# First chunk of a relu² attention and hard-swish MLP kernel: z and v are fetched ahead of the stores, ScalarE rounds v, and GpSimd's queue fetches the weights

## The chip, the cores and the metric

The kernel runs on one core of one Trainium2 chip. The metric is the device time of an execution in microseconds (us), and lower is better. Three runs of the kernel before took 1998.2, 1998.15 and 1996.16 us, a median of 1998.15 us. One more execution was profiled.

The engines go by the names of the profile. PE is TensorE (PEld its weight loads), DVE is VectorE, ACT is ScalarE, POOL is GpSimd, and SP is SyncE, which here only issues DMAs. Each engine, and each queue that issues DMAs, works through its own list of instructions in order.

## The reference

The computation has two stages, and the output of the first is the input of the second:

```python
B, S, D, DQK, DFF = 4, 3008, 256, 64, 2048
scores = (1.0 / S) * np.matmul(z, z.transpose(0, 2, 1))
attn = np.maximum(scores, 0.0) ** 2
x = (u * np.matmul(attn, v)).reshape(B * S, D)
h = x @ w_in
g = h * np.clip(h + 3.0, 0.0, 6.0) / 6.0
out = g @ w_out
```

u, v and z are float32. The two weight matrices arrive as float64 and are read as pairs of 32-bit words.

## The kernel before

**Precision.** Every operand of a matmul is kept as two float32r parts, a rounded high part (names that end in h) and the rest (l), and every product is taken as three matmuls: l by h, h by l, h by h. `split` makes the parts: ACT rounds the high part with a copy, and DVE subtracts it from the raw value. For z the parts lie in one tile each: `zx` and `zy` hold the high part in one half of the partitions and the rest in the other.

**Chunks and pairs.** For each of the four batches the 3008 columns of the scores are cut into six chunks `c` of 512 columns (the last has 448), so there are 24 chunks, and the 3008 rows into twelve pairs `p` of 2 x 128 rows. `scores(b, c, p)` makes one pair: four matmuls `s<-...` into one of two PSUM buffers, Relu on ACT (`rt`, L320), its square rounded on ACT (`ah`, L329), in the first chunk its unrounded square also on ACT (`r`, L330), and the rest on DVE (`al`, L340). `attend` (function `av`) then multiplies with v: twelve matmuls `o<-...`. The scores are symmetric: what is needed again in a later chunk is stored to DRAM by `keep` (`d<-r`, L257, two DMAs of a pair), and for the later chunk it comes back by four loads (`l<-d`, L240) and a transpose on DVE (`rm`, L271) in place of matmuls.

**The MLP** is cut into units, `up(q)` (twelve matmuls `h<-...`) and `down(q)` (twelve matmuls `y<-...`) for q = 0 to 7 of each chunk. They begin at pair 28 of all, counted from 0 (`FIRST = 28`, in the third chunk), and follow the attention of the pairs in a fixed proportion of about 1.4 units to a pair. The units of the first chunk come in the order up 0, up 1, down 0, up 2, down 1, ... up 7, down 6, down 7.

**The weights** come in sixteen pieces (w_in 0 to 7 and w_out 0 to 7, in the order in which the units of the first chunk use them). A piece is fetched by one 512 KB DMA (`wraw`, L152), and eight DVE instructions and one ACT copy turn it into its two parts: L101, L106, L110, L114, L119 and L123, and then, after the same six of the next piece, L131 and L133. This work is a generator, and the main loop takes some steps of it at a time:

```python
def weight_work(n):
    for _ in range(n):
        next(w_ops, None)

def weight_needed(w):
    while w not in ready:
        next(w_ops)
```

`weight_work` stands ahead of `attend` in every pair: 2 steps in the first chunk, 4 in the next, 5 from pair 28 of all on. `weight_needed` stands ahead of each unit of the first chunk and takes whatever steps are missing until the unit's piece is done.

**What sets the order.** The program order is written out by hand (`tc.manual_schedule()`), and each engine gets its instructions in that order. Tiles wait for the last users of their buffer: the pool `rpool` (tag `r`) has five buffers for `rt`, `r`, `rm`, `y` and the two `wraw` in flight. A DMA on SP's queue is issued once the eighth DMA before it on that queue has landed.

**The first chunk** (L561 to L608) has loads that later chunks do not have: z and v of batch 0. `fetch_z(0, k)` loads a raw z chunk through SP; for k > 1 two more loads through POOL's queue bring the high parts, which a DMA from float32 to float32r rounds. `fetch_v(0, p)` loads raw v through SP and a second, rounded copy `vh` through POOL's queue. The fetches run up to four pairs ahead of their use and stand between the stores of `keep`. Before the loop the first two weight pieces are fetched (`weight_work(1)`).

Of the kernel before, what the change touches and what calls it, by code (L numbers as in the profile page):

```python
# [15 lines left out]
P = 128  # L16
CH = 512
NCH = 6
# [12 lines left out]
def relu2_attention_then_hswish_mlp(  # L31
# [43 lines left out]
    def split(hi, lo, raw, rounded=False):  # L75
        if not rounded:
            nc.scalar.copy(out=hi, in_=raw)  # L77
        nc.vector.tensor_tensor(out=lo, in0=raw, in1=f(hi), op=ALU.subtract)  # L78
# [69 lines left out]
    def fetch_w(kind, q):  # L148
        _, _, src, cols = w_piece(kind, q)
        if wide:  # L150
            raw = rpool.tile([P, 2, D, 2], U32, tag="r", name="wraw")
            nc.sync.dma_start(  # L152
                out=raw.rearrange("p k n w -> p k (n w)"),
                in_=src[:, :, 2 * cols.start:2 * cols.stop],
            )
        else:
            raw = rpool.tile([P, 2, D], F32, tag="r", name="wraw")
            nc.sync.dma_start(out=raw, in_=src[:, :, cols])
        raws["w", kind, q] = raw

    raws = {}
# [3 lines left out]
    def fetch_v(b, p):  # L165

        if b == 0 and p < NPAIR - 1:
            raw = vpool.tile([P, 2, D], F32, tag="vl", name="vraw")
        else:
            raw = stg.tile([P, 2, D], F32, tag="stg", name="vraw")  # L170
        vh = vpool.tile([P, 2, D], F32R, tag="vh", name="vh")
        vt[b, p] = vh
        raws["v", p] = raw
        j0 = p * 2 * P
        for dst, queue in ((raw, nc.sync), (vh, nc.gpsimd))[:1 if b else 2]:
            if p < NPAIR - 1:
                queue.dma_start(
                    out=dst, in_=v[b, j0:j0 + 2 * P, :].rearrange("(r q) d -> q r d", q=P)
                )
            else:  # L180
                queue.dma_start(out=dst[:, 0, :], in_=v[b, j0:j0 + P, :])
                for h in range(2):
                    queue.dma_start(out=dst[64 * h:64 * h + 64, 1, :], in_=v[b, j0 + P:S, :])

    def split_v(b, p):
        vh, raw = vt[b, p], raws.pop(("v", p))
        vl = vpool.tile([P, 2, D], F32R, tag="vl", name="vl")
        split(vh, vl, raw, rounded=b == 0)
        vt[b, p] = (vh, vl)

    def fetch_z(b, k):
# [327 lines left out]
# [3 lines that stand above are left out]
# [39 lines left out]
    with tc.manual_schedule():  # L561
# [3 lines left out]
        split_z(0, 0)  # L565
        fetch_z(0, 1)
        fetch_v(0, 1)
        weight_work(1)
        split_v(0, 0)
        split_z(0, 1)  # L570
        scores(0, 0, 0)
        fetch_z(0, 2)
        fetch_v(0, 2)
        scores(0, 0, 1)
        fetch_v(0, 3)
        g_done = 2
        to_fetch += [(b, c, p) for b, c, p in pairs if p // 2 < c]
        g_turned = [2]
        for i, (b, c) in enumerate(chunks):
            ahead = b + 1 if c == NCH - 1 and b + 1 < B else None  # L580
            for p in range(NPAIR):
                g = i * NPAIR + p
                lead = 2 if g < FIRST else 1
                if i == 0:
                    if p + 1 < NPAIR:
                        split_v(0, p + 1)
                    if p % 2 == 0 and p // 2 + 2 < NCH:
                        split_z(0, p // 2 + 2)
# [4 lines left out]
                    fetch_mirrored()  # L593
                if p < NPAIR - 1:
                    turn_next()
                if i == 0:
                    if p + 4 < NPAIR:
                        fetch_v(0, p + 4)
                    if p % 2 == 0 and p // 2 + 3 < NCH:
                        fetch_z(0, p // 2 + 3)  # L600
                    if p == 6:
                        load_u(*chunks[0])
                        load_u(*chunks[1])
                maybe_split()
                if g >= FIRST:
                    weight_work(5)
                elif p < NPAIR - 2:
                    weight_work(4 if i else 2)  # L608
                if ahead and p < NPAIR - 1:
                    if p:  # L610
# [61 lines left out]
```

## Time and profile before

| | |
|---|---|
| Median of three runs | 1998.15 us |
| The profiled execution | 1999.87 us, of which 1998.1 us lie between its first and last instruction (the span) |
| PE busy in the span | 1960.8 us, 98% |
| DVE, ACT, POOL busy | 1280.7, 987.3 and 14.2 us |
| Mean granted clock of PE | 0.992 of full speed |
| Data moved by DMA | 178.14 MB |

The profile counts PE as busy while a matmul is in flight, and the matmuls overlap, so the count of matmuls in a stretch (the x behind the busy time) says more than the busy time. At full clock one matmul with 512 columns follows another after 0.227 us (twelve in 2.72 us), so 50 us have room for 220. The granted clock has two levels, 2.4 GHz (1.00) and 1.2 GHz (0.50); a stretch with both shows a value between. In the timeline a row gives the start, the duration, the engine, the line, the tiles, and in brackets how long the engine was idle ahead of it and who ended that. Rows of SPq are DMA issues on SP's queue.

### The profile page before, as it was taken

The numbers are of one execution on the slowest core, as the hardware profiler recorded it, in microseconds if no ns is written. First come the engines' busy times: TensorE is split into PE (matmuls) and PEld (weight loads), VectorE is DVE, ScalarE is ACT, GpSimd is POOL, SyncE is SP. The second block draws the span as 40 slices with busy tenths as digits, with TensorE's granted clock in tenths as the row PEclk, the third lists the DMA queues.
The fourth block names the chain that finished last, engine by engine and source line by source line (L and its number), as shares of the span: only waits on it lengthen the run. The fifth ranks groups of instructions, "written<-read, shape, count | busy, mean of one in ns | idle before, by whom it ended". The sixth has DMA issues, their size and how long they took to land.

```text
span 1998.1 us, 22059 instructions
## 1 busy us (share of the span) xinstructions
PE 1960.8 (98%) x8688; PEld 1637.4 (82%) x8688; DVE 1280.7 (64%) x1277; ACT 987.3 (49%) x1057; POOL 14.2 (1%) x26
## 2 busy tenths in 40 slices
PE   7899999999999999999999999999999999999999
PEld 5677788788888888888888888888888888888888
DVE  6798766676556566577565565657756565665654
ACT  6665444465444444456454454444555544444444
POOL 2000000000000000000000000000000000000000
PEclk8899999999999999999999999999999999999999
DMA  9754232424323233253332232324342223332300
GB/s 260 201 159 110 64 82 71 113 74 116 82 64 81 72 74 93 51 127 91 95 82 82 62 90 56 98 65 106 93 116 61 83 61 92 74 82 60 94 10 20
DMA packets 403271, 178.14 MB, mean 89 GB/s; under 512 B 250080, under 2 KB 385248, under 8 KB 403168
## 3 DMA queue, kind: packets, MB, share of 16 engines
q1 hardware_dynamic: 399232, 172.55, 34.3%
q0 software_dynamic: 3936, 4.20, 1.0%
q8 instruction: 68, 1.11, 0.2%
q14 instruction: 35, 0.29, 0.1%
HBM read 104.07 MB, written 72.61 MB: 88 GB/s over the span
## 4 chain that ended last, share of the span: by engine, by line
PE 89%; DVE 4%; DMA 3%; ACT 2%; issue 1%; SPq 1%; DVEq 0%; ACTq 0%
PE o L73 34%; PE h L73 24%; PE y L73 24%; PE s L73 7%; DMA zraw<-in_zz_dram 1%; DVE rm L271 1%; DMA vraw<-in_v_dram 1%; DVE al L287 1%; DVE rt L421 1%; ACT rt L420 0%; SPq L240 0%; ACT gh L77 0%; ACT rt L320 0%; DVE gl L78 0%; DMA d<-r 0%
## 5 line engine op out<-in xcount | busy, mean ns | idle before, releaser
L421 DVE SCALAR_TENSOR_TENSOR rt<-rt,h 128x1024 f32<-128x1024 f32 (+1 forms) x192 | 229.9, 1197 | 419.9 <-ACT rt L420 419.6
L420 ACT ACTIVATE rt<-h,three 128x1024 f32<-128x1024 f32 (+1 forms) x192 | 210.9, 1099 | 548.4 <-PE h L73 545.6
L73 PE MATMUL o<-ah,vl 128*128 128x512 f32 (+1 forms) x1152 | 448.5, 389 | 9.7 <-DVE vl L78 3.7
L73 PE MATMUL o<-ah,vh 128*128 128x512 f32 (+1 forms) x1152 | 447.6, 389 | 0.0
L73 PE MATMUL o<-al,vh 128*128 128x512 f32 (+1 forms) x1104 | 430.3, 390 | 7.8 <-DVE al L287 6.4
L73 PE MATMUL y<-gh,w_out_l 128*128 128x512 f32 (+1 forms) x768 | 296.2, 386 | 1.8 <-DVE w_out_l L133 1.7
L73 PE MATMUL y<-gl,w_out_h 128*128 128x512 f32 (+1 forms) x768 | 296.3, 386 | 1.0 <-DVE gl L78 1.0
L73 PE MATMUL h<-xh,w_in_l 128*128 128x512 f32 (+1 forms) x768 | 295.9, 385 | 0.0
L73 PE MATMUL y<-gh,w_out_h 128*128 128x512 f32 (+1 forms) x768 | 295.9, 385 | 0.0
L73 PE MATMUL h<-xl,w_in_h 128*128 128x512 f32 (+1 forms) x768 | 295.8, 385 | 0.0
L73 PE MATMUL h<-xh,w_in_h 128*128 128x512 f32 (+1 forms) x768 | 295.8, 385 | 0.0
L78 DVE TENSOR_TENSOR gl<-rt,gh 128x1024 fp32r<-128x1024 f32 (+1 forms) x192 | 230.6, 1201 | 80.5 <-ACT gh L77 77.9
L73 PEld LDWEIGHTS o<-ah,vl 128*128 128x128 f32 x1152 | 218.4, 190 | 57.6 <-ACT ah L285 5.8
L77 ACT CAST gh<-rt 128x1024 fp32r<-128x1024 f32 (+1 forms) x192 | 197.2, 1027 | 123.5 <-DVE rt L421 123.3
L73 PEld LDWEIGHTS o<-ah,vh 128*128 128x128 f32 x1152 | 218.6, 190 | 40.9
L73 PEld LDWEIGHTS o<-al,vh 128*128 128x128 f32 x1104 | 209.2, 190 | 51.5 <-DVE al L287 9.8
L320 ACT ACTIVATE rt<-s 128x1024 f32<-128x1024 f32 x168 | 171.2, 1019 | 131.9 <-PE s L73 126.9
L332 DVE TENSOR_TENSOR r<-rt 128x1024 f32<-128x1024 f32 (+1 forms) x140 | 169.9, 1214 | 95.8 <-ACT rt L320 95.8
L340 DVE TENSOR_TENSOR al<-r,ah 128x1024 fp32r<-128x1024 f32 x140 | 170.9, 1221 | 22.2 <-ACT r L330 8.7
L73 PEld LDWEIGHTS y<-gh,w_out_l 128*128 128x128 f32 x768 | 144.2, 188 | 29.9 <-DVE w_out_l L133 1.3
L73 PEld LDWEIGHTS y<-gl,w_out_h 128*128 128x128 f32 x768 | 144.2, 188 | 28.6 <-DVE gl L78 2.0
L287 DVE TENSOR_TENSOR al<-rm,ah 128x1024 fp32r<-128x1024 f32 (+1 forms) x120 | 141.1, 1176 | 40.0 <-ACT ah L285 39.9
(51 smaller groups left out, 1808.7 us busy)
## 6 DMA issues: line engine op xcount, KB each, us to landing
d<-r SPq DMA_DIRECT2D x220, 256.0 KB, 2.9
l<-d SPq DMA_DIRECT2D x320, 128.0 KB, 3.2
l<-d SPq DMA_DIRECT2D x160, 112.0 KB, 2.8
vraw<-in_v_dram SPq DMA_DIRECT2D x44, 256.0 KB, 3.4
u<-in_ut_dram SPq DMA_DIRECT2D x20, 512.0 KB, 4.3
out_dram<-y SPq DMA_DIRECT2D x40, 256.0 KB, 3.2
zraw<-in_zz_dram SPq DMA_DIRECT2D x24, 256.0 KB, 3.7
wraw<-in_w_in_dram SPq DMA_DIRECT2D x8, 512.0 KB, 4.5
```

Source lines behind the costliest of these rows:

```text
L73: nc.tensor.matmul(out, lhsT=lhsT, rhs=rhs, start=start, stop=stop)
L77: nc.scalar.copy(out=hi, in_=raw)
L78: nc.vector.tensor_tensor(out=lo, in0=raw, in1=f(hi), op=ALU.subtract)
L271: nc.vector.transpose(out=rn.rearrange("p r (k e) -> p r k e", e=32), in_=t[:, :n // 32].rearrange("p k (r e) -> p r k e", r=2),)
L287: nc.vector.tensor_tensor(out=al[:, :, :n], in0=rn, in1=f(ah[:, :, :n]), op=ALU.subtract)
L320: nc.scalar.activation(out=rn, in_=s[:, :, :n], func=AF.Relu, scale=1.0 / S)
L332: nc.vector.tensor_tensor(out=r2_of, in0=r_of, in1=r_of, op=ALU.mult)
L340: nc.vector.tensor_tensor(out=l_of, in0=r2_of, in1=h_of, op=ALU.subtract)
L420: nc.scalar.activation(out=rn, in_=h, func=AF.Relu, bias=three)
L421: nc.vector.scalar_tensor_tensor(out=rn, in0=rn, scalar=6.0, in1=h, op0=ALU.min, op1=ALU.mult)
```

## The change

It has four parts. (1) In the first chunk `fetch_v` no longer loads the rounded copy `vh` through POOL's queue; `split_v` lets ACT round it, as in the later batches. (2) z 2 and 3 and v 2 and 3 are fetched ahead of the first scores, z 4 and 5 at the start of pairs 0 and 1, and v 4 and later at the start of the pair, all ahead of that pair's stores. (3) The sixteen weight loads go through POOL's queue. (4) `weight_work(1)` before the loop is gone, and pair 0 of the first three chunks takes no step of the weights' work (`0 < p`). Loads of u move from pair 6 to pair 7.

```diff
@@ fetch_w
-            nc.sync.dma_start(
+            nc.gpsimd.dma_start(
                 out=raw.rearrange("p k n w -> p k (n w)"),
                 in_=src[:, :, 2 * cols.start:2 * cols.stop],
             )
...
@@ fetch_v
-        for dst, queue in ((raw, nc.sync), (vh, nc.gpsimd))[:1 if b else 2]:
-            if p < NPAIR - 1:
-                queue.dma_start(
-                    out=dst, in_=v[b, j0:j0 + 2 * P, :].rearrange("(r q) d -> q r d", q=P)
-                )
...
+        if p < NPAIR - 1:
+            nc.sync.dma_start(
+                out=raw, in_=v[b, j0:j0 + 2 * P, :].rearrange("(r q) d -> q r d", q=P)
+            )
...
@@ split_v
-        split(vh, vl, raw, rounded=b == 0)
+        split(vh, vl, raw)
@@ main
         fetch_v(0, 1)
-        weight_work(1)
+        fetch_z(0, 2)
+        fetch_z(0, 3)
+        fetch_v(0, 2)
+        fetch_v(0, 3)
         split_v(0, 0)
         split_z(0, 1)
         scores(0, 0, 0)
-        fetch_z(0, 2)
-        fetch_v(0, 2)
         scores(0, 0, 1)
-        fetch_v(0, 3)
...
                 if i == 0:
+                    if p + 4 < NPAIR:
+                        fetch_v(0, p + 4)
+                    if p < 2:
+                        fetch_z(0, p + 4)
...
-                if i == 0:
-                    if p + 4 < NPAIR:
-                        fetch_v(0, p + 4)
-                    if p % 2 == 0 and p // 2 + 3 < NCH:
-                        fetch_z(0, p // 2 + 3)
-                    if p == 6:
-                        load_u(*chunks[0])
-                        load_u(*chunks[1])
+                if i == 0 and p == 7:
+                    load_u(*chunks[0])
+                    load_u(*chunks[1])
                 maybe_split()
                 if g >= FIRST:
                     weight_work(5)
-                elif p < NPAIR - 2:
+                elif 0 < p < NPAIR - 2:
                     weight_work(4 if i else 2)
```

PE's instructions stand in the same order as before. The change moves instructions on DVE, ACT, SP and POOL; the three places that the prediction speaks of follow.

On ACT, in the middle of the first chunk, the list before goes as follows (rt, ah and r are one pair's scores, w_in_h is a weight piece):

```order
L320 ACTIVATE rt<-s 128x1024
L329 ACTIVATE ah<-rt 128x1024
L330 ACTIVATE r_263<-rt 128x8x4x32
L117 CAST w_in_h<-t_198 128x2x256
L320 ACTIVATE rt<-s 128x1024
L329 ACTIVATE ah<-rt 128x1024
L330 ACTIVATE r_306<-rt 128x8x4x32
```

The same stretch of ACT's list now (the line numbers behind the change are one lower):

```order
L77 CAST vh<-vraw 128x512
L319 ACTIVATE rt<-s 128x1024
L328 ACTIVATE ah<-rt 128x1024
L329 ACTIVATE r_309<-rt 128x8x4x32
L77 CAST vh<-vraw 128x512
L319 ACTIVATE rt<-s 128x1024
L328 ACTIVATE ah<-rt 128x1024
L329 ACTIVATE r_346<-rt 128x8x4x32
```

One rounding of v has come in for every pair.

On DVE, early in the fourth chunk's attention, where the first chunk's last MLP units run, the list before goes as follows (rt and gl belong to the unit up 7, the steps of the weights' work finish the piece w_out 6; the piece w_in 7 was finished in the stretch ahead of this one):

```order
L271 STREAM_TRANSPOSE rm<-l 128x1024
L114 SCALAR_TENSOR_TENSOR t_1590<-wraw,t_1590 128x512
L119 TENSOR_SCALAR wraw<-t_1590 128x512
L123 SCALAR_TENSOR_TENSOR w_out_l<-wraw 128x512
L131 TENSOR_TENSOR t_1490<-t_1490,w_out_h 128x512
L133 TENSOR_TENSOR w_out_l<-t_1490,w_out_l 128x512
L421 SCALAR_TENSOR_TENSOR rt<-rt,h 128x1024
```

The same place of DVE's list now:

```order
L270 STREAM_TRANSPOSE rm<-l 128x1024
L101 TENSOR_SCALAR t_1623<-wraw 128x512
L106 SCALAR_TENSOR_TENSOR t_1623<-wraw,t_1623 128x512
L110 TENSOR_SCALAR wraw<-wraw 128x512
L114 SCALAR_TENSOR_TENSOR t_1623<-wraw,t_1623 128x512
L119 TENSOR_SCALAR wraw<-t_1623 128x512
L123 SCALAR_TENSOR_TENSOR w_out_l<-wraw 128x512
L131 TENSOR_TENSOR t_1504<-t_1504,w_in_h 128x512
L133 TENSOR_TENSOR w_in_l<-t_1504,w_in_l 128x2x256
L101 TENSOR_SCALAR t_1657<-wraw 128x512
L420 SCALAR_TENSOR_TENSOR rt<-rt,h 128x1024
```

Nine steps stand where five stood: `weight_work` takes five, and `weight_needed`, called for the unit up 7, four more, and among them are now those that finish w_in 7.

One pair later on DVE, ahead of the unit down 6, the list before (xl are the parts of the next chunk's x, the two steps finish w_out 7):

```order
L271 STREAM_TRANSPOSE rm<-l 128x1024
L78 TENSOR_TENSOR xl_1701<-u,xh_1700 128x512
L78 TENSOR_TENSOR xl_1705<-u,xh_1704 128x512
L131 TENSOR_TENSOR t_1590<-t_1590,w_out_h 128x512
L133 TENSOR_TENSOR w_out_l<-t_1590,w_out_l 128x512
L287 TENSOR_TENSOR al<-rm,ah 128x1024
```

The same place now:

```order
L270 STREAM_TRANSPOSE rm<-l 128x1024
L78 TENSOR_TENSOR xl_1691<-u,xh_1690 128x512
L78 TENSOR_TENSOR xl_1695<-u,xh_1694 128x512
L106 SCALAR_TENSOR_TENSOR t_1657<-wraw,t_1657 128x512
L110 TENSOR_SCALAR wraw<-wraw 128x512
L114 SCALAR_TENSOR_TENSOR t_1657<-wraw,t_1657 128x512
L119 TENSOR_SCALAR wraw<-t_1657 128x512
L123 SCALAR_TENSOR_TENSOR w_out_l<-wraw 128x512
L131 TENSOR_TENSOR t_1623<-t_1623,w_out_h 128x512
L133 TENSOR_TENSOR w_out_l<-t_1623,w_out_l 128x512
L131 TENSOR_TENSOR t_1657<-t_1657,w_out_h 128x512
L286 TENSOR_TENSOR al<-rm,ah 128x1024
```

Eight steps stand where two stood, and the seventh of them finishes w_out 6.

## Rows read from the trace of the kernel before

**Rows 1.** The view of stretches over the whole span: the stretch, PE's busy time (instructions), the same of PEld, DVE, ACT and POOL, then PE's granted clock, the DMA share and GB/s.

```profile
0.00:50.00 50.00, 37.77 (x133) 29.18 (x134) 29.99 (x41) 31.60 (x34) 14.21 (x26) 0.86 1.13 260
50.00:100.00 50.00, 42.70 (x165) 33.74 (x164) 38.04 (x53) 31.53 (x34) 0.00 (x0) 0.86 0.70 201
...
200.00:300.00 100.00, 96.94 (x423) 78.57 (x422) 67.16 (x66) 45.34 (x47) 0.00 (x0) 1.00 0.32 73
```

**Rows 2.** The timeline of PE in the first chunk, the matmuls ahead of which PE stood idle longest.

```profile
32.01 0.47 PE L73 MATMUL s<-zy,zx 128*128 128x512 f32 x1 [2.28 <-issue]
34.98 0.77 PE L73 MATMUL o<-ah,vl 128*128 128x512 f32 x1 [1.49 <-DVE vl L78]
...
54.89 0.77 PE L73 MATMUL s<-zy,zx 128*128 128x512 f32 x1 [3.90 <-issue]
...
72.16 0.47 PE L73 MATMUL o<-ah,vl 128*128 128x512 f32 x1 [2.21 <-DVE vl L78]
```

**Rows 3.** The timeline of DVE, the two splits of z that waited longest.

```profile
30.50 0.68 DVE L78 TENSOR_TENSOR zy<-zraw,zx 64x512 fp32r<-64x512 f32 x1 [4.74 <-DMA zraw<-in_zz_dram]
...
53.39 0.68 DVE L78 TENSOR_TENSOR zy<-zraw,zx 64x512 fp32r<-64x512 f32 x1 [6.35 <-DMA zraw<-in_zz_dram]
```

**Rows 4.** The timeline of SP's queue: two loads of z and the block of eight loads that stands ahead of the second.

```profile
18.76 0.78 SPq L201 DMA_DIRECT2D zraw<-in_zz_dram  x1
...
40.38 6.86 SPq L240 DMA_DIRECT2D l<-d  x8
...
48.04 0.47 SPq L201 DMA_DIRECT2D zraw<-in_zz_dram  x1
```

**Rows 5.** The chain of waits, in order of time: two runs of twelve matmuls (start, us, what, count).

```profile
34.98 5.09 PE o L73 x12
...
41.00 2.74 PE o L73 x12
```

**Rows 6.** The view of stretches again, in steps of 5 us around the second long wait for z, with the columns of rows 1.

```profile
55.00:60.00 5.00, 3.82 (x9) 2.54 (x10) 4.93 (x7) 3.40 (x4) 0.00 (x0) 0.50 1.04 337
60.00:65.00 5.00, 5.00 (x16) 3.93 (x15) 3.55 (x6) 0.46 (x2) 0.00 (x0) 0.66 0.93 292
```

**Rows 7.** The timeline of ACT in the first chunk: the scores of pair 3 (at 19.77), a wait for a store, one whole pair with a weight copy behind it, and the end of the scores of pair 11.

```profile
19.77 1.03 ACT L320 ACTIVATE rt<-s 128x1024 f32<-128x1024 f32 x1 [3.07 <-PE s L73]
...
27.91 1.06 ACT L330 ACTIVATE r<-rt 128x1024 f32<-128x1024 f32 x1 [2.31 <-DMA d<-r]
...
41.04 1.03 ACT L320 ACTIVATE rt<-s 128x1024 f32<-128x1024 f32 x1 [1.94 <-PE s L73]
...
43.06 1.04 ACT L330 ACTIVATE r<-rt 128x1024 f32<-128x1024 f32 x1
44.01 0.60 ACT L117 CAST w_in_h<-t 128x512 fp32r<-128x512 f32 x1
...
44.74 1.03 ACT L320 ACTIVATE rt<-s 128x1024 f32<-128x1024 f32 x1
...
66.60 1.04 ACT L330 ACTIVATE r<-rt 128x1024 f32<-128x1024 f32 x1
```

**Rows 8.** The view of one source line, L257 (the stores), up to 70 us: time from issue to landing.

```profile
DMA to landing us min/median/max: 2.6/5.1/10.4
```

**Rows 9.** The timeline of PE at the start of the third chunk.

```profile
132.97 0.50 PE L73 MATMUL o<-al,vh 128*128 128x512 f32 x1 [0.69 <-DVE al L287]
```

**Rows 10.** The timeline of DVE from 200 us on: steps of the weights' work (L101 to L133) among the rest.

```profile
201.85 0.65 DVE L131 TENSOR_TENSOR t<-t,w_in_h 128x512 f32<-128x512 f32 x1
...
203.14 0.42 DVE L101 TENSOR_SCALAR t<-wraw 128x512 uint32<-128x512 uint32 x1
203.59 0.69 DVE L106 SCALAR_TENSOR_TENSOR t<-wraw,t 128x512 uint32<-128x512 uint32 x1
...
204.66 1.21 DVE L421 SCALAR_TENSOR_TENSOR rt<-rt,h 128x1024 f32<-128x1024 f32 x1
...
209.30 0.65 DVE L114 SCALAR_TENSOR_TENSOR t<-wraw,t 128x512 f32<-128x512 f32 x1
...
212.39 1.21 DVE L421 SCALAR_TENSOR_TENSOR rt<-rt,h 128x1024 f32<-128x1024 f32 x1
214.72 1.22 DVE L78 TENSOR_TENSOR gl<-rt,gh 128x1024 fp32r<-128x1024 f32 x1 [1.12 <-ACT gh L77]
...
219.32 0.68 DVE L131 TENSOR_TENSOR t<-t,w_out_h 128x512 f32<-128x512 f32 x1
```

**Rows 11.** The timeline of PE over the same time: the first matmul of the units down 5, up 7, down 6 and down 7 of the first chunk.

```profile
203.49 0.39 PE L73 MATMUL y<-gh,w_out_l 128*128 128x512 f32 x1
...
206.21 0.39 PE L73 MATMUL h<-xh,w_in_l 128*128 128x512 f32 x1
...
212.62 0.47 PE L73 MATMUL y<-gh,w_out_l 128*128 128x512 f32 x1 [0.80 <-DVE w_out_l L133]
...
220.79 0.50 PE L73 MATMUL y<-gh,w_out_l 128*128 128x512 f32 x1 [0.89 <-DVE w_out_l L133]
```

**Rows 12.** The timeline of ACT: the Relu of a unit up.

```profile
190.41 1.12 ACT L420 ACTIVATE rt<-h,three 128x1024 f32<-128x1024 f32 x1 [2.25 <-PE h L73]
```

**Rows 13.** The first step of the weights' work on DVE, from the timeline.

```profile
19.48 0.42 DVE L101 TENSOR_SCALAR t<-wraw 128x512 uint32<-128x512 uint32 x1
```

**Rows 14.** The view of the tile vh up to 140 us, the loads on POOL's queue: time from issue to landing.

```profile
DMA to landing us min/median/max: 6.4/7.6/14.5
```

More of the change, by code (lines that the diff above doesn't have):

```diff
@@ L157, in fetch_w @@
             raw = rpool.tile([P, 2, D], F32, tag="r", name="wraw")
-            nc.sync.dma_start(out=raw, in_=src[:, :, cols])
+            nc.gpsimd.dma_start(out=raw, in_=src[:, :, cols])
         raws["w", kind, q] = raw
@@ L174, in fetch_v @@
         j0 = p * 2 * P
-        for dst, queue in ((raw, nc.sync), (vh, nc.gpsimd))[:1 if b else 2]:
-            if p < NPAIR - 1:
-                queue.dma_start(
-                    out=dst, in_=v[b, j0:j0 + 2 * P, :].rearrange("(r q) d -> q r d", q=P)
-                )
[L180 to L183, printed above, removed]
+        if p < NPAIR - 1:
+            nc.sync.dma_start(
+                out=raw, in_=v[b, j0:j0 + 2 * P, :].rearrange("(r q) d -> q r d", q=P)
+            )
+        else:
+            nc.sync.dma_start(out=raw[:, 0, :], in_=v[b, j0:j0 + P, :])
+            for h in range(2):
+                nc.sync.dma_start(out=raw[64 * h:64 * h + 64, 1, :], in_=v[b, j0 + P:S, :])
     def split_v(b, p):
```

## The prediction

> **What bounds the kernel now.** I read first the view of stretches. At full clock 50 us have room for 220 matmuls; the first 50 us hold 133, the next 165, and from 200 us on PE runs 423 in 100 us with the clock at 1.00 [rows 1]. So later PE is the bound and gives nothing back: whatever is won or lost early stays to the end. Then the timeline of PE for the first chunk: idle 2.28 and 1.49 us around 32 us, 3.90 us at 54.89, 2.21 us at 72.16 [rows 2]. The two longest of them are put down to "issue"; DVE's rows tell what it was: the splits of z 3 and z 5 waited 4.74 and 6.35 us for the raw load [rows 3]. SP's rows tell why: z 3 was issued only at 18.76 and landed 11.65 us later (it ends DVE's wait at 30.4), and z 5 stood behind a block of eight loads that held the queue for 6.86 us and was issued at 48.04 [rows 4]. Each such hole also costs clock: twelve matmuls took 5.09 us after the first, 2.74 us later [rows 5]; after the second the granted clock was 0.50, and 0.66 in the 5 us behind it [rows 6], some 16 matmuls at 0.425 in place of 0.227 us.
>
> At last I read DVE and PE from 200 to 221 us, where the change moves most rows of DVE's list. There DVE is full: its only idle times are those of 1.1 us ahead of gl, and PE waits 0.80 and 0.89 us for a weight piece that DVE has only just finished [rows 10, 11].
>
> **Part A, the first chunk.** z 3 to z 5 and v leave the store-bound place in SP's queue, so both waits for z go; twelve loads of 256 KB leave POOL's queue. In their place ACT gets a rounding of v per pair. What is late next is ACT. The scores of pair 3 start at 19.77, when PE has made them [rows 7], and that stays, since all ahead of it waits for PE and the first loads. A pair on ACT with one copy of 0.60 behind it takes 44.74 - 41.04 = 3.70 us [rows 7] (the copy there is a weight's, of the same size as v's). PE needs 16 x 0.227 = 3.63 us a pair, so the two run level. Pair 11 then starts at 19.77 + 8 x 3.70, plus two weight copies of 0.60, = 50.6, and its scores end 3.06 us later (41.04 to 43.06 + 1.04) at 53.6; before, they ended at 67.64 [rows 7].
>
> A wait stays: ACT's tiles need a buffer that a store has left (such a wait took 2.31 us at 27.91 [rows 7]). Stores of a pair come in twos and land 5.1 us after issue in the median (2.6 to 10.4) [rows 8]. ACT comes back to the buffer some 4.3 us after a pair's end, about when its store lands; I take 0 for most pairs. But the block of eight loads still stands ahead of the store of pair 7: by the same spacing pair 6 ends at 34.0, its store and the block hold SP until about 42, pair 7's store follows the v load and lands near 48, and the scores of pair 9 want the buffer at 44.6. That is 3.2 us, so pair 11 ends at 56.8. From there to the next matmul of PE it took 72.16 - 67.64 = 4.52 us before [rows 2, 7], by DVE's order, which is the same now: 61.3. Part A gives 72.16 - 61.3 = **-10.8 us**. Bounds: -14.0 without the wait for the store, -7 if every other store (4 of them) costs ACT another 1 us.
>
> The Trainium skill speaks against this part: by "DMA: Bandwidth & Descriptors", section "Queues, rings and completion order", each DMA engine takes packets from its queues in turn. By that rule two weight loads on POOL's queue no longer stand behind the stores but take half of the engines from them; the rows of the stores (2.6 to 10.4 us) [rows 8] do not say for which queue they waited. By it the stores of pairs 2 and 3 would land some 2 us later, and the sum would be about 1 us higher; I leave it inside the bounds.
>
> **Part B, the start of the third chunk.** Pair 0 there no longer takes four steps of the weights' work ahead of the `al` for which PE waited 0.69 us [rows 9]: **-0.7 us** (0 to -0.7). In the second chunk the same skip meets no wait of PE: 0.
>
> **Part C, the last weight pieces.** The steps left out are 3 in the first chunk and 4 each in pair 0 of the second and third, 11 in all. They are not gone: from pair 28 on each pair still takes five, so eleven are left over for the very end, where DVE is full, and `weight_needed` has to pull them ahead of the unit that wants them. That is what DVE's list shows: nine steps where five stood, then eight where two stood. Worked out on the clock of the profile before, from 201.85:
>
> - The first group of five is L114 to L133 now, which took 212.39 - 209.30 = 3.09 us, in place of 204.66 - 201.85 = 2.81 [rows 10]; all behind it is 0.28 us later, and down 5, whose piece ends this group, starts at 204.94 in place of 203.49 [rows 11].
> - Nine steps follow at 209.30 + 0.28 = 209.58. The eight up to the L133 of w_in 7 take 3.09 + (204.66 - 203.14) = 4.61 us [rows 10]: 214.2. Up 7 on PE, which ran at 206.21 [rows 11], waits for that: PE is idle for 6.5 us.
> - PE's clock is then at its lower level: twelve matmuls in 5.1 us [rows 5], 219.3. ACT's Relu 1.12 us [rows 12], then DVE from rt to gl 214.72 - 212.39 = 2.33 us, from gl over al and rm to the end of xl 219.32 - 214.72 = 4.60 us [rows 10], and the seven steps to the L133 of w_out 6, 4.61 - 0.45 = 4.16 us. Down 6 starts at 231.5 in place of 212.62 [rows 11].
> - Down 6 and the o behind it are 24 matmuls, 5.44 us, and 16 x 0.198 = 3.2 us more at the lower level. Down 7 starts at 240.1 in place of 220.79 [rows 11].
>
> Part C costs **+19.3 us**. With the clock at 2.40 GHz throughout, up 7 ends at 216.9 and down 7 starts at 234.6: +13.8, the lower bound. I take the first value, since both idle times (6.5 us, then 8 us) are longer than those of 3.90 us behind which the clock did fall [rows 2, 6].
>
> **Part D, the weights through POOL's queue.** SP's queue loses sixteen loads; where it is late in the second chunk it waits for ACT's results and not for its own issues, so I put the gain at 0 (at best the few tenths by which a store leaves earlier). The loads have POOL's queue alone once z is in, and leave as soon as their buffer is free.
>
> **Sum.** 1999.87 (the profiled execution) - 10.8 - 0.7 + 19.3 = 2007.7 us. The median of the runs is 1.72 us below that execution, so **2006 us**.
>
> **Rivals.**
>
> *The two cancel.* The clock does not fall behind the late pieces (+13.8), and the stores never hold ACT (-14.0 - 0.7): 1998.15 - 0.9 = 1997.3. For it: the clock did not fall after the 1.49 us idle time at 34.98 alone, but after both. Against it: the idle times in part C are far longer. Values up to about 2002 belong here too.
>
> *Faster, the other side.* The late pieces cost only their DVE time: if DVE reaches the place at 201.85 ahead of PE by what the skipped steps freed, the eleven steps cost 11 x 0.6 = 6.6 us, and the sum is 1998.15 - 10.8 - 0.7 + 6.6 = 1993. It decides for this if w_in 7 is done within about 1 us of PE's arrival at up 7. Against it: between the third chunk's start and 201.85 both lists give DVE the same number of steps in each pair, so it gains no lead there.
>
> *The weight loads come late as well.* Before, the first two pieces were fetched ahead of everything, and their first step ran at 19.48 [rows 13]. Now the fetch waits for a buffer that the scores of pair 1 leave (near 16 us, an estimate from the 3.7 us that a pair takes back from pair 3 at 19.77), and the step comes behind the `al` of pair 3, near 22, with the split of z 3 behind it. Loads on POOL's queue took 6.4 to 14.5 us [rows 14]: with 7.6 us DVE waits 2 us, which the pairs in hand cover; with 14.5 PE waits some 4 us for z 3 and pair 4, 2010 us. For it: the piece has twice the bytes of a vh. Against it: POOL's queue is empty by then.
>
> By the Trainium skill ("SBUF — State Buffer", section "Who interferes with whom") this is likelier than the rows make it: DVE instructions with one source, such as L101, may hold the port through which POOL writes its descriptors. By that rule a load leaves up to 0.42 us later, the length of an L101 [rows 13]; no wait of that kind is seen in the rows here, so the price stays at zero in the sum.
>
> **How the numbers follow.** What a measurement of this kernel can tell from no change is about 0.2%, 4 us. Forecast (parts A to C as worked out, 2002 to 2011): 0.65. Late loads on top: 0.08. Cancelled, 1994 to 2002: 0.17. Faster: 0.10. So slower 0.73, same 0.17, faster 0.10. The range goes from 1996, below the sum with the better end of every term, to 2013, the forecast with 4 us of late loads and part A at its poorer end halfway; the forecast's own is 2002 to 2011.
>
> **What would show it.** Part A: no wait of DVE's z splits for `zraw` over 1 us, the matmul that stood at 72.16 near 61, ACT busy nearly throughout from 20 to 57 us. Part C: two idle times of PE over 5 us ahead of up 7 and down 6 of the first chunk, put down to DVE's w_in_l and w_out_l at L133, with a granted clock below 1.00 behind each, some 190 to 230 us into the span. The forecast is wrong if those waits are under 2 us each, or if PE's matmul of 72.16 comes later than 65.

## The result, and the profile after

The changed kernel takes 2020.62 us (median of 4 runs, 2018.03 to 2021.3), the kernel before on the same chip 1998.18 us: a ratio of 1.0111, 95% interval 1.0099 to 1.0124, some 22 us slower. Forecast were 2006 us, 8 us slower, with a range from 1996 to 2013; the result lies outside it. The profiled execution took 2021.3 us, its span is 2019.5 us.

The view of stretches, with the columns of [rows 1]: the first 50 us hold 23 matmuls more than before and the next 50 us 9 more, at a clock of 1.00 and 0.93 in place of 0.86 twice. Then the gain goes: 162 from 100 to 150 us, where 195 ran before, and 346 at a clock of 0.91 from 200 to 300 us, where 423 ran.

```profile
0.00:50.00 50.00, 39.44 (x156) 30.39 (x156) 32.22 (x44) 36.06 (x43) 6.73 (x15) 1.00 0.91 235
50.00:100.00 50.00, 42.91 (x174) 34.33 (x175) 37.06 (x51) 36.53 (x41) 2.89 (x4) 0.93 0.68 182
100.00:150.00 50.00, 41.36 (x162) 30.25 (x161) 37.87 (x52) 26.28 (x29) 2.89 (x4) 0.97 0.52 125
...
200.00:300.00 100.00, 83.14 (x346) 67.35 (x345) 61.20 (x66) 38.03 (x40) 0.72 (x1) 0.91 0.25 62
```

The timeline of PE in the first chunk, which answers to [rows 2]. The holes ahead of z 3 and z 5 are gone; the last row is the matmul that stood at 72.16. It comes 9.6 us earlier.

```profile
30.03 0.50 PE L73 MATMUL o<-ah,vl 128*128 128x512 f32 x1 [2.72 <-DVE vl L78]
...
53.75 0.80 PE L73 MATMUL o<-ah,vl 128*128 128x512 f32 x1 [4.60 <-DVE vl L78]
...
62.57 0.50 PE L73 MATMUL o<-ah,vl 128*128 128x512 f32 x1 [0.45 <-DVE vl L78]
```

ACT's timeline tells what the two idle times left are: waits for buffers that stores have to leave, 3.34 and 5.57 us. The first row is the start of pair 3's scores, which stood at 19.77 before [rows 7].

```profile
17.08 1.02 ACT L319 ACTIVATE rt<-s 128x1024 f32<-128x1024 f32 x1
...
23.99 1.03 ACT L319 ACTIVATE rt<-s 128x1024 f32<-128x1024 f32 x1 [3.34 <-DMA d<-r]
...
49.58 1.06 ACT L329 ACTIVATE r<-rt 128x1024 f32<-128x1024 f32 x1 [5.57 <-DMA d<-r]
```

The timeline of PE at the end of the first chunk's MLP, which answers to [rows 11]: down 5, up 7, the o behind it, down 6, down 7. Two waits for DVE's last subtract of a weight piece (L133), 6.44 and 9.98 us.

```profile
205.35 0.50 PE L73 MATMUL y<-gh,w_out_l 128*128 128x512 f32 x1 [0.44 <-DVE w_out_l L133]
...
214.81 0.77 PE L73 MATMUL h<-xh,w_in_l 128*128 128x512 f32 x1 [6.44 <-DVE w_in_l L133]
...
219.94 0.39 PE L73 MATMUL o<-ah,vl 128*128 128x512 f32 x1
...
232.82 0.77 PE L73 MATMUL y<-gh,w_out_l 128*128 128x512 f32 x1 [9.98 <-DVE w_out_l L133]
...
240.24 0.39 PE L73 MATMUL y<-gh,w_out_l 128*128 128x512 f32 x1
```

Twelve matmuls of up 7 take 219.94 - 214.81 = 5.13 us; the stretches around both waits show the lower clock (0.52 and 0.60, columns as above).

```profile
214.00:220.00 6.00, 5.19 (x13) 4.11 (x14) 1.00 (x2) 0.00 (x0) 0.00 (x0) 0.52 0.01 3
...
232.00:238.00 6.00, 5.18 (x15) 4.13 (x16) 4.14 (x5) 0.00 (x0) 0.00 (x0) 0.60 0.31 85
```

What the forecast puts at nothing lies between the first chunk and these units. The timeline of ACT in the second chunk, the end of a pair's scores and a weight's copy, ahead of the next pair's scores; before, the copy follows at once, and now it waits some 2 us. First the kernel before, then the changed one.

```profile
101.05 1.04 ACT L330 ACTIVATE r<-rt 128x1024 f32<-128x1024 f32 x1
102.00 0.60 ACT L117 CAST w_in_h<-t 128x512 fp32r<-128x512 f32 x1
```

```profile
90.47 1.05 ACT L329 ACTIVATE r<-rt 128x1024 f32<-128x1024 f32 x1
93.57 0.63 ACT L117 CAST w_out_h<-t 128x512 fp32r<-128x512 f32 x1 [2.05 <-DVE t L114]
```

DVE at the same time: `al` needs ACT's r (released at 91.5), L114 stands behind `al`, and ACT's copy behind L114. Then DVE waits 1.86 us for ACT. At this place the two work by turns.

```profile
91.72 1.22 DVE L339 TENSOR_TENSOR al<-r,ah 128x1024 fp32r<-128x1024 f32 x1
92.86 0.68 DVE L114 SCALAR_TENSOR_TENSOR t<-wraw,t 128x512 f32<-128x512 f32 x1
...
97.19 1.23 DVE L339 TENSOR_TENSOR al<-r,ah 128x1024 fp32r<-128x1024 f32 x1 [1.86 <-ACT r L329]
```

PE then waits for `al`. Between 85 and 110 us it does so for more than 1 us three times, of which two are shown; the kernel before has no such wait there.

```profile
89.73 0.50 PE L73 MATMUL o<-al,vh 128*128 128x512 f32 x1 [1.71 <-DVE al L339]
...
107.96 0.50 PE L73 MATMUL o<-al,vh 128*128 128x512 f32 x1 [1.70 <-DVE al L339]
```

To see where time goes in each kernel, I took from the timelines of PE the first matmul of five places: pair 0 of the second chunk (its first o), pair 9 of the second, pair 2 of the third, down 5 and down 7 of the first chunk. The columns are the times between them, in us, of one profiled execution each; the third row and those after it are kernels of the experiments below.

| kernel | to pair 0 of chunk 2 | to pair 9 | to pair 2 of chunk 3 | to down 5 | to down 7 |
|---|---|---|---|---|---|
| before | 77.01 | 32.69 | 18.20 | 75.59 | 17.30 |
| changed | 65.87 | 36.18 | 23.90 | 79.40 | 34.89 |
| steps skipped alone | 75.11 | 35.42 | 21.32 | 78.39 | 34.26 |
| weights on POOL's queue alone | 74.25 | 32.67 | 24.96 | 74.49 | 17.29 |
| ACT rounds v alone | 66.07 | 32.64 | 16.53 | 76.56 | 17.35 |
| order of loads alone | 71.56 | 32.64 | 18.25 | 75.59 | 17.34 |
| changed, steps back | 66.02 | 32.64 | 23.15 | 75.88 | 17.33 |
| same, weights on SP's queue | 61.28 | 32.64 | 16.50 | 76.34 | 17.36 |
| changed, one step more | 64.16 | 32.64 | 24.78 | 76.19 | 33.86 |
| steps back, one more | 66.69 | 36.40 | 22.82 | 80.03 | 17.78 |
| changed, weights on SP's queue | 70.61 | 35.42 | 21.31 | 78.43 | 34.50 |
| steps back, two more | 68.67 | 32.73 | 25.51 | 76.11 | 16.33 |
| changed, eleven steps made up late | 65.31 | 36.15 | 23.76 | 83.94 | 24.17 |
| changed, twelve made up late | 64.60 | 36.15 | 24.25 | 82.63 | 17.41 |
| steps back, later first fetch | 64.40 | 32.64 | 22.71 | 75.89 | 17.35 |

Changed against before: -11.1, +3.5, +5.7, +3.8, +17.6, and +1.95 behind down 7: the +21.4 us of the two spans. The table tells places, the ratios tell sizes: the execution profiled of the kernel before took 1999.87 us, 1.7 us over the median of its runs and 2 to 4 us over those of the later comparisons, so sums over a row can differ from a ratio by some us.

### The profile page after: what moved, and what is told of

Same layout as the page of the kernel before. It is cut to its first block, busy times and chain, and to the rows that moved or that the text cites. A ratio compares the mean times of both kernels' runs of the same rounds, so it can differ in the third digit from the quotient of the medians.

```text
span 2019.5 us, 22042 instructions
## 1 busy us (share of the span) xinstructions
PE 1964.2 (97%) x8688; PEld 1638.9 (81%) x8688; DVE 1281.2 (63%) x1277; ACT 993.4 (49%) x1069; POOL 16.1 (1%) x28
## 4 chain that ended last, share of the span: by engine, by line
PE 85%; DVE 5%; ACT 4%; DMA 3%; issue 2%; SPq 0%; DVEq 0%; ACTq 0%
PE o L73 31%; PE h L73 24%; PE y L73 24%; PE s L73 6%; DMA d<-r 2%; ACT rt L319 1%; DMA zraw<-in_zz_dram 1%; DVE rt L420 1%; ACT r L329 1%; ACT rt L419 1%; DVE rm L270 1%; DMA vraw<-in_v_dram 1%; DVE al L286 1%; ACT ah L328 1%; DVE gl L78 1%
## 5 line engine op out<-in xcount | busy, mean ns | idle before, releaser
L73 PEld LDWEIGHTS h<-xh,w_in_l 128*128 128x128 f32 x768 | 144.9, 189 | 36.3 <-issue 6.8
```

Source lines behind the costliest of these rows:

```text
L73: nc.tensor.matmul(out, lhsT=lhsT, rhs=rhs, start=start, stop=stop)
```

## The experiments

A step is one `yield` of the weights' work, some 0.4 to 0.7 us of DVE; eight of them finish a piece, and a pair of the second chunk issues a group of four. Which of the eight steps stands first in a group is called the phase here, the number of steps by which the work is behind the kernel before the lag. Each kernel was timed against runs of the kernel before on the same chip (medians 1995.7 to 1997.9 us); ratios are to those.

### The four parts, each alone

**The skipped steps alone.** The kernel before, with

```diff
-        weight_work(1)
...
-                elif p < NPAIR - 2:
+                elif 0 < p < NPAIR - 2:
```

> The kernel before with nothing but the eleven steps skipped (no step ahead of the first scores, none in pair 0 of a chunk); the loads, the vh load and the weights' queue stay as before. Theory (the skip alone makes both losses): 1998.2 + 11.5 + 17.6 = 2027 us (2022 to 2030). Rival (the second chunk's loss needs the changed loads or queue): 1998.2 + 17.6 = 2016 us (2013 to 2019).

2023.98 us, ratio 1.0138 (1.0123 to 1.0153): +27.5 us. The skip alone costs more than the whole change does. Its row in the table shows both places: +2.7, +3.1 and +2.8 us in the three columns of the second chunk and after, +17.0 ahead of down 7.

**The weights' queue alone.** The kernel before, with `nc.gpsimd` in place of `nc.sync` in `fetch_w`.

> The kernel before with nothing but the weights' sixteen loads moved to GpSimd's queue. Theory (loads on a queue of their own are moved at once, beside the loads of z and v and beside the stores, and hold these up: with the eleven steps back, the two queues differ by 10.35 us): 5 to 10 us slower than before, 2003 us where that takes 1996.5 (2000 to 2008), with the first loads of z and v landing some 3 to 6 us later. Rival (it costs only where the loads of z and v stand early in SP's queue, as in the changed kernel): 1996.5 us (1994 to 1998.5).

2002.03 us, ratio 1.0022 (1.0012 to 1.0032): +4.4 us. The queue costs, a little less than was expected, and not where I expected it: the first chunk is 2.8 us shorter, and 6.8 us are lost between pair 9 of the second chunk and pair 2 of the third. Nor do the first loads land later, as I expected: the loads of v that are issued in the first 10 us land after 9.2 us in the median, before after 11.5.

**The rounding alone.** The kernel before, with

```diff
-        for dst, queue in ((raw, nc.sync), (vh, nc.gpsimd))[:1 if b else 2]:
+        for dst, queue in ((raw, nc.sync), (vh, nc.gpsimd))[:1]:
...
-        split(vh, vl, raw, rounded=b == 0)
+        split(vh, vl, raw)
```

> The kernel before with nothing but v's high part rounded by ScalarE in the first chunk, in place of the load on GpSimd's queue. Theory of the queues (twelve loads of 256 KB less beside the loads of z): z 3 lands earlier, but z 5 still stands behind the block of eight loads, so 2 to 5 us faster: 1993 us where the kernel before takes 1996.5 (1990.5 to 1995). Rival (ScalarE gets 0.6 us a pair more and is late next): 1996.5 to 2000 us.

1987.92 us, ratio 0.9957 (0.9942 to 0.9971): -8.6 us, more than I expected, although DVE's wait for z 5 stays (5.97 us, where it was 6.35 [rows 3]).

**The order of the loads alone.** The kernel before, with the changed order of `fetch_z`, `fetch_v` and `load_u`; v's high part still comes by a second load.

> The kernel before with nothing but the loads of z, v and u in the changed kernel's order; the steps, the weights' queue and the second load of v's high part as before. Theory (both waits of DVE for z are a matter of SP's order): most of the first chunk's gain, 8 us faster than before: 1988.5 us where that takes 1996.5 (1985 to 1992). Rival (the loads are bound by the engines and not by their place; without the rounding the bytes stay): 1994 to 1998 us.

1994.17 us, ratio 0.9985 (0.9975 to 0.9994): -3.0 us. The theory misses; the time lies at the edge of the rival's range. The waits for z that [rows 3] show do go: what is left of all six splits is one wait, in the view of waits of DVE in the first 75 us (in all, times, longest):

```profile
DVE zy L78 <- DMA zraw<-in_zz_dram: 0.6, 1, 0.6
```

But the loads only start earlier, there are no fewer bytes, and other waits grow: ACT waits for stores 13.2 us in these 75 us in place of 9.8, the longest time 7.1 us in place of 3.9. The view of DMA issues in the same 75 us (KB each, median us to landing), first for the kernel before, then for the order alone, then for the rounding alone:

```profile
d<-r SPq DMA_DIRECT2D x19, 256.0 KB, 5.1
vraw<-in_v_dram SPq DMA_DIRECT2D x11, 256.0 KB, 5.6
...
zraw<-in_zz_dram SPq DMA_DIRECT2D x6, 256.0 KB, 5.8
```

```profile
d<-r SPq DMA_DIRECT2D x19, 256.0 KB, 4.8
vraw<-in_v_dram SPq DMA_DIRECT2D x11, 256.0 KB, 8.5
...
zraw<-in_zz_dram SPq DMA_DIRECT2D x6, 256.0 KB, 12.8
```

```profile
d<-r SPq DMA_DIRECT2D x19, 256.0 KB, 4.4
vraw<-in_v_dram SPq DMA_DIRECT2D x11, 256.0 KB, 4.9
...
zraw<-in_zz_dram SPq DMA_DIRECT2D x6, 256.0 KB, 4.1
```

Put earlier, z takes 12.8 us to land in place of 5.8. Without the 3 MB of the second load of v all three kinds land sooner. So the waits for z came from the DMA engines, which [rows 1] show full in the first 50 us (a share of 1.13), as much as from a late place in SP's queue.

The four alone add up to -8.6 - 3.0 + 4.4 + 27.5 = +20.3 us; together they cost 22.

### The steps: phase and lateness

**All steps back.** The changed kernel, with

```diff
         fetch_v(0, 1)
+        weight_work(1)
...
-                elif 0 < p < NPAIR - 2:
+                elif p < NPAIR - 2:
```

> The changed kernel with the eleven skipped steps of the weights' work put back where the kernel before has them (the first step ahead of the first scores, two in pair 0 of the first chunk, four in pair 0 of the second and third); the order of the loads, ScalarE's rounding of v and the weights' queue stay changed. Theory (the skipped steps cause both losses: 11.5 us from pair 11's first matmul to down 5, 17.6 us from down 5 to down 7): what is left is the gain of the first chunk, 9.6 us, so 1988.5 us (1986 to 1992), DVE's first-chunk order as before and no wait of ScalarE's weight copies of 2 us each in the second chunk. Rival (the loss in the second chunk comes from the weights' loads on POOL's queue or from the new order of the loads): only the tail's 17.6 us goes, 2003 us (2000 to 2006).

1995.32 us, ratio 0.9997 (0.9988 to 1.0006). Against the changed kernel some 23 us go, and both losses with them: the second column is 32.64 us again, the last 17.33. But it is not 1988.5: of the first chunk's 11 us the third column takes 5 back. The theory of the steps holds, and a second cause is left, which the next section finds.

**One step more.** The changed kernel, lag ten in place of eleven.

```diff
                 elif 0 < p < NPAIR - 2:
                     weight_work(4 if i else 2)
+                elif i == 0 and p == 10:
+                    weight_work(1)
```

> The changed kernel with one single step more, in pair 10 of the first chunk, where none stood: lag ten in place of eleven. Theory (phase: with lag eleven DVE's multiply at L114, which ScalarE's copy at L117 needs, is first in its group of four, right behind the al of the pair, and the subtract at L131 in the same group flushes the copy into ScalarE's list ahead of the next pair's scores, so that each copy waits some 2 us and ScalarE and DVE work by turns): one step more makes it last in its group and the copy goes behind the next pair's scores. The seven waits of L117 for L114 fall under 0.5 us each, the 11.5 us of the second chunk go, the tail keeps its loss less one step: 2008.5 us (2005 to 2012). Rival (the lag itself, or the queue, or the buffers hold the second chunk up): one step in eleven is worth 0.4 to 1.5 us, 2019 to 2020 us.

2010.41 us, ratio 1.0073 (1.0056 to 1.009). By the ratios 1.0111 - 1.0073 that is 7.6 us less, give or take 4, for one step of 0.7 us. The last column of the table falls by only 1.0 us, so most of it is not the lateness of the last pieces: the place of L114 in its group, not the lag, makes the loss in the second chunk. The view of groups, ACT's copies between 72 and 145 us (busy, mean ns, idle time ahead of them), first of the kernel before, then of the changed kernel, then with one step more:

```profile
L117 ACT CAST w_in_h<-t 128x512 fp32r<-128x512 f32 x4 | 2.5, 617 | 3.2 <-DVE t L114 3.2
L117 ACT CAST w_out_h<-t 128x512 fp32r<-128x512 f32 x3 | 1.8, 612 | 0.3 <-DVE t L114 0.3
```

```profile
L117 ACT CAST w_out_h<-t 128x512 fp32r<-128x512 f32 x4 | 2.5, 622 | 11.4 <-DVE t L114 11.4
L117 ACT CAST w_in_h<-t 128x512 fp32r<-128x512 f32 x3 | 1.9, 622 | 6.1 <-DVE t L114 6.1
```

```profile
L117 ACT CAST w_out_h<-t 128x512 fp32r<-128x512 f32 x3 | 1.8, 615 | 4.0 <-DVE t L114 4.0
L117 ACT CAST w_in_h<-t 128x512 fp32r<-128x512 f32 x3 | 1.8, 614 | 1.2 <-DVE t L114 1.2
```

3.5 us of waits before are 17.5 in the changed kernel and 5.2 with one step more (5.4 with all steps back); not every one fell under 0.5 us, as I had expected.

**All steps back and one more; and two more.** The same edit with one and with two steps, on the kernel with all steps back.

> The changed kernel with all eleven steps back, and one more in pair 10 of the first chunk: one step ahead of the kernel before. By the theory of the phase this is the bad place again (L114 first in its group behind the al, L131 fourth), though more of the weights' work is done earlier: the waits of L117 for L114 of some 2 us come back, and it takes 5 to 8 us longer than the kernel with the eleven steps back: 2002 us where the kernel before takes 1996 (1999 to 2004). Rival (what counts is how far the weights' work is ahead): 1994 to 1995.5 us, a little faster.

> All eleven steps back, and two more in pair 10 of the first chunk. Theory of the phase: L114 is last in its group, no wait of L117 for it; with two steps less at the end it is as fast as the kernel with the steps back or up to 1.5 us faster: 1994.5 us where the kernel before takes 1996 (1992.5 to 1996.5). Rival (each step put into the first chunk costs there, as ScalarE or DVE is full): like the one with one step more.

One more: 2001.46 us, ratio 1.0026 (1.0016 to 1.0036), 6 us (give or take 3) slower than without it, with the waits of L117 back:

```profile
L117 ACT CAST w_in_h<-t 128x512 fp32r<-128x512 f32 x4 | 2.5, 623 | 9.7 <-DVE t L114 9.7
...
L117 ACT CAST w_out_h<-t 128x512 fp32r<-128x512 f32 x3 | 1.9, 622 | 6.8 <-DVE t L114 6.8
```

Two more: 1996.94 us, ratio 0.9999 (0.9989 to 1.0009), as fast as without. A step that brings the work ahead costs 6 us, the next one gives most of them back: the phase does that, and how far the work is ahead does not. Two steps ahead bring nothing (up to 1.5 us was expected).

**Made up late.** The changed kernel, with the eleven steps made up from pair 28 to 38; then with twelve.

```diff
-                    weight_work(5)
+                    weight_work(5 if g > FIRST + 10 else 6)
```

> The changed kernel with the eleven skipped steps made up late: six steps a pair in place of five from pair 28 to pair 38, so the second chunk keeps the bad phase and the last pieces come nearly as early as before. Theory (two separate losses, 7.6 us by phase in the second chunk, some 16 us by lateness ahead of up 7 and down 6): the waits of over 5 us of PE at L133 go to under 1.5 us, the waits of L117 for L114 stay: some 7 us over the kernel before, 2003 us where that takes 1996 (2000 to 2006). Rival (the late stretch is lost to DVE's sum of work there, whatever the order): 2010 us or more.

> The late make-up with twelve steps in place of eleven: seven in pair 28, six in pairs 29 to 38. With eleven the subtract at L133 of w_out piece 6 fell by one step into the next pair's group, behind two transposes, al, gl and xl, and PE waited 8.52 us for it ahead of down 6. Theory (the lateness costs what each piece is late for its unit, so one step is worth the whole wait): the wait of 8.52 us falls under 1.5 us and the time by 7 to 9 us against eleven steps, 2002 us where the kernel before takes 1996.5 (1999.5 to 2004.5). Rival (DVE's sum of work in that stretch is what is lost): one step more changes less than 1 us, 2010 us.

Eleven: 2010.34 us, ratio 1.0075 (1.0053 to 1.0096), as the rival had it. Twelve (seven in pair 28): 2004.19 us, ratio 1.0034 (1.0021 to 1.0048). The wait of PE ahead of down 6 tells why, first with eleven, then with twelve:

```profile
225.99 0.77 PE L73 MATMUL y<-gh,w_out_l 128*128 128x512 f32 x1 [8.52 <-DVE w_out_l L133]
```

```profile
216.87 0.47 PE L73 MATMUL y<-gh,w_out_l 128*128 128x512 f32 x1 [0.92 <-DVE w_out_l L133]
```

With eleven the one subtract that down 6 needs fell into the next pair's group. One step of 0.7 us took some 8 us away by the ratios (7.1 by the two spans), so what is lost there is the lateness of single pieces, not DVE's sum of work. The 6.8 us that are left are about the phase's, which this edit keeps (36.15 us in the second column); but the steps made up also stand ahead of down 5 (82.63 us, where the changed kernel has 79.40), and the runs do not separate the two.

### The queue

**Weights on SP's queue.** The changed kernel, and the one with the steps back, each with `nc.sync` in `fetch_w` again.

> The changed kernel with the sixteen weight loads issued from SP's queue again. Theory (the queue is worth nothing, the phase of the steps does it): 2020.6 us (2018 to 2023), the waits of L117 for L114 as they are. Rival (the loads of 512 KB on a queue of their own take the DMA engines from the stores that free ScalarE's buffers, seen as its waits for d<-r of 3.8 us): those waits go, 2012 us or less.

> All eleven steps back, and the weights' loads issued from SP's queue again. With the steps back the first chunk's gain of 10 us fell to 6 us over the mirrored pairs, where ScalarE waited 3.2 us once for a store and the stores landed 3.7 us after issue in the median of 80 to 110 us (2.9 in the kernel before, whose weight loads stand behind them in the same queue). Theory (loads on POOL's queue share the DMA engines with the stores and hold them up): the stores land in 2.9 us again and it is 2 to 5 us faster than with POOL's queue: 1991 us where the kernel before takes 1996 (1989 to 1993.5). Rival (the same bytes move, the stores are bound by the engines whichever queue they share): 1995 us (1994 to 1997).

With the steps back: 1984.97 us, ratio 0.9946 (0.9926 to 0.9966), 10.8 us faster than before, faster than both kernels and by more than the theory gave. With the steps skipped: 2020.0 us, ratio 1.0122 (1.0107 to 1.0137), no difference to the changed kernel, as the theory had it, though not for its reason: the queue is worth something, as the first of the two shows. The table shows how both can be. The column from pair 9 to pair 2 is 16.5 to 18.3 us with the right phase on SP's queue, 21.3 with the wrong phase, 22.7 to 25.5 wherever the weights come on POOL's queue: either cause is enough to lose most of it. And without the early first step the first weight loads stand in SP's queue at 20.94, between the stores: DVE waits 5.41 us for the first of them and PE 4.21 us behind it (27.36), and ACT waits 6.43 us for a store at 50.40. The first chunk, 4.7 us longer than in the changed kernel, loses what the later columns gain.

The DMA issues from 76 to 112 us, first with the steps back on POOL's queue, then on SP's. In the median stores land in 3.8 us with the weights on POOL's queue and in 2.8 on SP's, the pieces of w_out in 5.3 and 4.1.

```profile
d<-r SPq DMA_DIRECT2D x15, 256.0 KB, 3.8
...
wraw<-in_w_out_dram POOLq DMA_DIRECT2D x2, 512.0 KB, 5.3
```

```profile
d<-r SPq DMA_DIRECT2D x13, 256.0 KB, 2.8
wraw<-in_w_out_dram SPq DMA_DIRECT2D x2, 512.0 KB, 4.1
```

On POOL's queue the chain of waits goes over three stores that took longer still, 5.5 to 6.0 us, each issued 0.3 us behind a weight load. Two of them, first POOL's timeline with the issues of the weights, then the chain:

```profile
93.63 0.72 POOL L152 DMA_DIRECT2D wraw<-in_w_in_dram  x1 [6.87 <-ACT r L329]
103.42 0.72 POOL L152 DMA_DIRECT2D wraw<-in_w_out_dram  x1 [9.06 <-ACT r L329]
```

```profile
93.92 6.03 DMA d<-r
...
103.70 5.52 DMA d<-r
```

The same shows at the start, in the issues of the first 10 us, five loads of v and five of z in both kernels: with two weight loads on POOL's queue, issued at 1.25 and 2.08, v lands 13.9 us after issue and z 12.2; with the same two in SP's queue behind the first two loads of z and of v, 10.8 and 9.6.

```profile
zraw<-in_zz_dram SPq DMA_DIRECT2D x5, 256.0 KB, 12.2
vraw<-in_v_dram SPq DMA_DIRECT2D x5, 256.0 KB, 13.9
wraw<-in_w_in_dram POOLq DMA_DIRECT2D x2, 512.0 KB, 8.9
```

```profile
zraw<-in_zz_dram SPq DMA_DIRECT2D x5, 256.0 KB, 9.6
vraw<-in_v_dram SPq DMA_DIRECT2D x5, 256.0 KB, 10.8
wraw<-in_w_in_dram SPq DMA_DIRECT2D x2, 512.0 KB, 10.1
```

**A later first fetch.** All steps back, POOL's queue, but `weight_work(1)` behind the first two `scores`.

> The changed kernel with the eleven steps back, on GpSimd's queue, but the first step (which fetches the first two pieces) put behind the first two scores in place of ahead of them. Theory (two thirds of what GpSimd's queue costs is lost where its first two loads run beside the first loads of z and v): the scores of pair 3 start near 15 us in place of 19.4, and 3 to 5 us of it stay to the end: 1991 us where the kernel before takes 1996.5 (1989 to 1993.5). Rival (the loads then run beside the first stores and hold them, and ScalarE with them, just as long; what counts is the later stores): 1995.5 us (1994 to 1998).

1991.57 us, ratio 0.9975 (0.9964 to 0.9985): 4 us of the 10 come back. The time is the theory's, its two thirds are not: the scores of pair 3 start on PE at 17.33 in place of 19.41 us, less than expected, and the third column, 22.71 us, hardly falls (23.15 with the steps back alone). So the larger part of the queue's cost is the later one, where weights and stores overlap.

## Why the prediction was wrong

Both signs that the prediction named for being wrong stayed away: the two waits of PE in part C are 6.44 and 9.98 us, and the matmul of 72.16 came at 62.57. They watched only places that had a price. Two terms put at nothing failed, the skip in the second chunk and the weights' queue.

**Part A (-10.8) had the right size, half a wrong reason and some luck.** The matmul of 72.16 came at 62.57, forecast 61.3. But the start of pair 3's scores, which was to stay at 19.77, came at 17.08, and the waits for stores, put at 3.2 us in all, took 3.34 and 5.57: the two errors nearly cancel. The rounding, the order and the old queue together gain 10.8 us in the end. But the step "The two longest of them are put down to 'issue'; DVE's rows tell what it was" stopped one view too early. The order alone takes both waits away and gains 3 us; the rounding, which takes loads from the DMA engines and adds work to ACT, gains 8.6 with one wait left. What I had costed as "ACT gets a rounding" was the larger gain.

**Part B (-0.7):** the matmul of [rows 9] came at 130.91 with no idle time ahead of it, as forecast; what the kernel as a whole gained by that, no run shows.

**"In the second chunk the same skip meets no wait of PE: 0."** This step failed. I looked for a wait of PE at the place of the skip, and took the rest of the chunk as unchanged. But skipping 7 steps by then shifts the groups of four by 3, and all of the chunk's groups stand differently: L114 moved from the second place to the first, behind `al`, with L131, which flushes the copy, in the same group. It costs 7.6 us (one step more), 6 us (one step too many) by two runs. The eleven steps as a whole, 18.6 us by parts B and C, cost 27.5 us alone, 23 in the changed kernel and 35 with its weights on SP's queue (2020.0 - 1984.97).

**Part C (+19.3) had the mechanism and the places right.** From down 5 the forecast had up 7 after 9.3 us, down 6 after 26.6 and down 7 after 35.2; measured are 9.5, 27.5 and 34.9. The clock fell behind the wait as in [rows 5, 6]. In time it was some 3.5 us too dear: the kernel with one step more lies 15.1 us above the one with all steps back, for which parts B and C give 18.6; the table's last column has 16.5 between these two and 17.6 between changed and before.

**Part D (0) is the other step that failed.** I looked at what the queue saves SP; the sharing, "some 2 us" for two stores and 1 us in all, I took from the first two loads alone and kept out of the sum. The fourteen other loads I did not price at all, though those of the second chunk run beside the stores that ACT waits for. Alone the queue costs 4.4 us, with the phase right 10.35 (1995.32 - 1984.97). The rule I weighed there, of the Trainium skill ("DMA: Bandwidth & Descriptors", section "Queues, rings and completion order"), is that an engine takes packets from its queues in turn. The landing times agree with it, since stores and weights both take longer where they overlap (2.8 to 3.8 and 4.1 to 5.3 us); the turns themselves no run shows. In the changed kernel the weights back on SP's queue gain nothing, so for this one kernel the 0 holds, but by luck: there SP's queue loses in the first chunk what it gains later.

So the parts do not simply add. By the ratios, one way from the kernel before to the changed one closes: loads and rounding on the old queue -10.8, the queue +10.2, the late pieces +15.2, the phase +7.6, in all +22.2 us. Forecast were -10.8, 0, +18.6 (parts B and C) and 0. The two zeros miss 17.8 us, the late pieces give 3.4 back, and that is the miss of 14 us. On another way, steps first, the queue's share is nothing and the steps' is 35 us; what each cost in the full change depends on the order in which they are counted.

Of the rivals none came true: no cancelling, no lead of DVE. The weight loads did not come late either; the first step ran at 21.31 us, and the split of z 3 behind it waited for nothing.

What stays open: why the first chunk is 2.8 us shorter with the weights on POOL's queue alone, though not in the other kernels. The first loads of v land sooner there (9.2 in place of 11.5 us); one profile each does not tell it from chance.

## What to carry to other kernels

Where work is dealt out in fixed portions between pairs of two engines that release each other, leaving out a portion moves every later one: look at where each instruction that another engine waits for stands in its portion, in the whole program and not only at the edit. A load given a queue of its own is not out of the way; here it ran beside the stores that ACT waits for, and with the steps in their place the queue that puts it behind them was the better one. Name as a sign of being wrong also the places that were priced at nothing. Before moving a late load forward, see whether the DMA engines have room for it: here leaving out bytes gained nearly three times what the order did.

## What was not expected of the hardware

Two loads of 512 KB on a second queue made the first five loads of v land 13.9 us after issue in place of 10.8, and those of z 12.2 in place of 9.6, and themselves landed in 8.9 in place of 10.1 us: the second queue was served at once, at the cost of the loads issued beside and behind it. And in the order alone z's landing rose from 5.8 to 12.8 us when it was issued earlier, though z 3 to z 5, the three that were moved, came in 11 to 20 us earlier than before.
